# Linear attention and two expert layers on one core: w_in loaded in rows of 128, q and k by heads in two transfers each, two quarters of a product by TensorE transposes, and a new order

## The chip, the cores and the metric

The kernel runs on one core of a Trainium2 chip. The metric is the device time of one execution in microseconds (us). The engines are TensorE (PE in the rows; PEld is its weight load), VectorE (DVE), ScalarE (ACT), GpSimd (POOL) and SyncE (SP), whose instruction stream does nearly all the loading by issuing DMAs.

## What is computed

The reference has three stages, each fed by the one before it.

```python
# 1: linear attention with decay, B=2, H=8, S=768, D=64, in blocks of 64 rows
intra = einsum('bhic,bhjc->bhij', qb, kb) * Dmask        # Dmask[h,i,j] = lam[h]**(i-j), i >= j
out   = einsum('bhij,bhjd->bhid', intra, vb) + einsum('bhid,bhde->bhie', qb * lam_pow, kv_state)
kv_state = lam**64 * kv_state + einsum('bhsd,bhse->bhde', kb * rev_pow, vb)
x = out.transpose(0, 2, 1, 3).reshape(1536, 512)
# 2: w_in [512, 2048] and w_out [2048, 512] are float64
h = x @ w_in
y = (h * clip(h + 3, 0, 6) / 6) @ w_out                  # [1536, 512]
# 3: soft mixture: phi [512, 32], w1 [8, 512, 1024], w2 [8, 1024, 512]
logits = y @ phi                                         # 32 slots, 4 for each of 8 experts
slots  = softmax(logits, over tokens).T @ y
slot_out[e] = relu(slots[e] @ w1[e]) @ w2[e]
result = softmax(logits, over slots) @ slot_out          # [1536, 512]
```

## The kernel before

**Tiling.** The attention works on chunks of 128 rows: twelve tiles `t`, six for each of the two batches. For each tile `load_qkv` (L412 to L430, issue in L419) loads q and k side by side into one tile `qk` of 128 partitions x 2 x 8 heads x 64, and v into `vd`, with one DMA of 256 KB for each of q, k and v. TensorE transposes q and k by pairs of heads into `pt` (`f_tr`, L793, four products each), ScalarE evicts them to `tr` (`f_ev`, L810), TensorE makes the scores `ps` (`f_sc`, L862), VectorE multiplies them by the decay table `dec` into `pm` (`f_pm`, L870), and TensorE makes the outputs `px` (`f_px`, L900 and L907) and the state's increment `pv` (`f_pv`, L883). `px` becomes `x`, the transposed input of the second stage, split in a high and a low part. In `x` a block `kt` of 128 rows holds the heads `kt` and `kt + 4`.

**The float64 matrices.** A piece of w_in (`load_w_in`, L433 to L441, issue in L438) is 128 rows x 512 columns of 8 bytes, 512 KB, in a tile `wraw`; there are 16, for four quarters of columns and four blocks `kt`. Since block `kt` of `x` holds the heads `kt` and `kt + 4`, its rows of w_in are two runs of 64, and each piece comes by two DMAs of 64 partitions. ScalarE and VectorE convert each piece to float32 (`convert`, L583, L590, L597, L604, tiles `tmp_i`; the same code converts w_out, loaded by `load_wo_raw` in 16 pieces `wo_raw`, tiles `tmp_o`, into `wo_f`), and it is split into `whi` (ScalarE, L630) and `wlo` (VectorE or GpSimd, L633). The product `h` (L1019) has 48 groups, four quarters by twelve tiles, each of twelve products of 128x512, done in two halves of six. ScalarE (L1033) and VectorE (L1039) evict it to `g`.

**The product w2s.** w_out is not multiplied by `g`; first w_out times phi is formed, `w2s`, in four quarters (`make_w2s`). It needs w_out transposed, and there are two ways for a quarter, chosen by the tuple `w2dma`. Before, all four quarters are in it: VectorE transposes blocks of 32 (`wb`, L710, two for a quarter), four DMAs of 128 KB for each of these move the blocks between partitions (`wq`, L723), and TensorE makes 64 products `w2p` (L735). The other way, which no quarter takes before, is four groups of four transposes on TensorE (`pwo`), an eviction of each by ScalarE (`wo_t`) and 32 products of twice the columns. The logits `lg` (L1125) need `g` transposed and use the VectorE way with moves `gq` (L1102, L1112).

**The end.** Softmax terms (`lr`, `pd`) follow; then the experts' weights are streamed in 64 DMAs of 512 KB (`e`, L1322, L1332, L1346) for the products `p` (L1540) and `po` (L1574), and the result is combined.

**What sets the order.** Nothing is scheduled on the chip or by a planner. The program makes a list of numbered operations, and the table `ORDER` says in which order their code is run; each engine executes its instructions in that order, and waits where an operand is late. `Plan.run` also uses modelled times, but only to decide which free buffer an operation takes. Loads have 4-KB slots in a ring of 50; a few of the moves can be issued by ScalarE instead of SP, those numbered in `BY_ACT`. SP issues all loads of q, k, v, w_in, w_out and `e` and nearly all moves in one stream, a DMA waiting there when its buffer is not free or when eight transfers are under way. `keep_on` (L544) fills TensorE with products that nobody reads.

## Time and profile before

| | before |
|---|---|
| median of 3 runs | 309.9 us (309.62 to 311.62) |
| the profiled execution | 310.75 us |
| its span | 308.9 us |
| TensorE busy | 277.1 us, 90% |
| VectorE busy | 198.8 us, 64% |
| ScalarE busy | 122.8 us, 40% |
| GpSimd busy | 36.3 us, 12% |
| moved by DMA | 78.67 MB, mean 255 GB/s |
| chain that ended last | PE 63%, DMA 17%, SP's issues 10% |

The span is the time from the first to the last instruction that the profiler recorded, and the execution's own time lies 1.85 us above it. Busy shares are averages over the whole span. The clock that TensorE was granted (PEclk) is given as a share of full speed; its two levels are 1.2 and 2.4 GHz. The DMA share is how busy the 16 transfer engines were on average; it can show a little over 1 where packets overlap. The chain of work that ended last follows the last instruction back to what released it, step by step.

### The profile page before, as it was taken

To read this page: it belongs to the slowest core of one execution; us is meant where nothing else is said; L and a number is where in the kernel's file an instruction comes from. 1 tells how busy PE (TensorE), PEld (TensorE's weight loads), DVE (VectorE), ACT (ScalarE), POOL (GpSimd) and SP (SyncE) were. 2 spreads that over 40 slices of the span, in tenths; PEclk is the share of its full clock that TensorE was granted. 3 is DMA by queue.
4 is the path that set the end of the run, shared out by engine and by line. 5 is a ranking of instruction groups with operands and counts; after the bars stand their busy time and mean duration, and the time that the engine had idled before them with its cause. 6 is when DMAs were issued, how large, how long until landed. Compare 5 with 4: busy or idle time off the path is not lost.

```text
span 308.9 us, 7313 instructions
## 1 busy us (share of the span) xinstructions
PE 277.1 (90%) x2956; PEld 210.1 (68%) x2956; DVE 198.8 (64%) x330; ACT 122.8 (40%) x235; POOL 36.3 (12%) x51
## 2 busy tenths in 40 slices
PE   6269994999879899999999999999999998979990
PEld 5268883878657788788667768668776756556670
DVE  3368894799946999998987796675633216213151
ACT  3454555988347657312131232224124241111240
POOL 4034210423202602000110010100000000000000
PEclk9578998899959999999999999999999999999997
DMA  7999999999996765667896768999799999999987
GB/s 145 221 234 210 208 213 179 241 293 317 219 215 181 249 181 153 168 155 191 194 262 162 205 152 197 227 306 358 243 334 417 395 408 342 389 407 407 313 262 235
DMA packets 79217, 78.67 MB, mean 255 GB/s; under 512 B 41800, under 2 KB 67920, under 8 KB 79184
## 3 DMA queue, kind: packets, MB, share of 16 engines
q1 hardware_dynamic: 76704, 76.37, 88.1%
q10 hardware_dynamic: 2480, 1.84, 2.1%
q8 instruction: 23, 0.38, 0.5%
q14 instruction: 10, 0.08, 0.1%
HBM read 60.36 MB, written 3.15 MB: 206 GB/s over the span
## 4 chain that ended last, share of the span: by engine, by line
PE 63%; DMA 17%; SPq 10%; DVE 4%; issue 1%; ACT 1%; POOLq 0%; DVEq 0%; ACTq 0%
PE h L1019 35%; SPq L419 5%; SPq L438 4%; DMA wo_raw<-in_moe_w_out_dram 4%; PE po L1574 4%; DMA e<-in_moe_w_dram 4%; PE lg L1125 3%; DMA qk<-in_q_dram 3%; PE p L1540 3%; PE pd L1240 3%; PE ps L862 3%; DMA wraw<-in_moe_w_in_dram 2%; PE pt L793 2%; PE px L907 2%; DMA qk<-in_k_dram 2%; DMA gq<-gb 2%
## 5 line engine op out<-in xcount | busy, mean ns | idle before, releaser
L1019 PE MATMUL h<-whi,x 128*128 128x512 f32 x384 | 124.1, 405 | 0.6 <-DVE g L1039 0.6
L1019 PEld LDWEIGHTS h<-whi,x 128*128 128x128 f32 x384 | 70.8, 191 | 17.6 <-issue 2.0
L1019 PE MATMUL h<-wlo,x 128*128 128x512 f32 x192 | 75.9, 395 | 0.0
L1033 ACT ACTIVATE g<-h,half_b 128x512 f32<-128x512 f32 x48 | 33.0, 688 | 53.1 <-PE h L1019 37.4
L1039 DVE SCALAR_TENSOR_TENSOR g<-g,h 128x512 f32<-128x512 f32 x48 | 32.6, 678 | 29.3 <-ACT g L1033 25.9
L1102 DVE STREAM_TRANSPOSE gb<-g 128x1024 f32<-128x1024 f32 x20 | 40.9, 2053 | 5.3 <-POOL vd L849 2.5
L1019 PEld LDWEIGHTS h<-wlo,x 128*128 128x128 f32 x192 | 36.6, 191 | 8.3
L793 PE MATMUL pt<-ident,qk 128*128 128x128 f32 x96 | 15.8, 308 | 13.8 <-DMA qk<-in_q_dram 13.8
L793 PEld LDWEIGHTS pt<-ident,qk 128*128 128x128 f32 x96 | 12.1, 155 | 17.4 <-DMA qk<-in_q_dram 8.0
L931 POOL TENSOR_TENSOR states<-states,lamq 64x256 f32<-64x256 f32 x16 | 10.7, 669 | 88.9 <-DVE states L944 80.7
L810 ACT COPY tr<-pt 128x512 f32<-128x512 f32 x24 | 13.6, 582 | 17.9 <-PE pt L793 9.5
L870 DVE TENSOR_TENSOR pm<-ps,dec 128x512 f32<-128x512 f32 x24 | 15.7, 681 | 7.2 <-ACT tmp_o L590 4.0
L862 PE MATMUL ps<-tr 64*128 64x128 f32 x192 | 15.9, 306 | 3.2 <-ACT tr L810 3.0
L862 PEld LDWEIGHTS ps<-tr 64*128 64x128 f32 x192 | 13.3, 207 | 7.1 <-ACT tr L810 3.5
L583 ACT ACTIVATE tmp_i<-wraw 128x512 f32<-128x512 f32 x16 | 10.5, 670 | 18.9 <-DMA wraw<-in_moe_w_in_dram 14.5
L1559 DVE STREAM_TRANSPOSE ht<-hsi 128x256 f32<-128x256 f32 x8 | 5.1, 651 | 19.6 <-ACT hsi L1551 19.6
L1540 PE MATMUL p<-e,hsi 128*32 128x256 f32 x256 | 15.2, 381 | 2.1 <-DMA e<-in_moe_w_dram 1.6
L710 DVE STREAM_TRANSPOSE wb<-wo_f 128x1024 f32<-128x1024 f32 x8 | 16.1, 2022 | 0.1
L849 POOL TENSOR_TENSOR vd<-qk,rev 128x512 f32<-128x512 f32 x10 | 11.0, 1112 | 42.8 <-DVE rev L535 12.8
L1574 PE MATMUL po<-e,ht 128*32 128x128 f32 (+1 forms) x384 | 15.4, 309 | 0.3 <-DMA e<-in_moe_w_dram 0.3
L633 POOL TENSOR_TENSOR wlo<-tmp_i,whi 128x512 fp32r<-128x512 f32 x8 | 11.2, 1419 | 25.4 <-ACT whi L630 25.3
L1574 PEld LDWEIGHTS po<-e,ht 128*32 128x32 f32 x384 | 11.1, 110 | 4.4 <-DMA e<-in_moe_w_dram 0.5
(115 smaller groups left out, 341.9 us busy)
## 6 DMA issues: line engine op xcount, KB each, us to landing
e<-in_moe_w_dram SPq DMA_DIRECT2D x64, 512.0 KB, 7.1
gq<-gb SPq DMA_DIRECT2D x76, 128.0 KB, 2.8
wraw<-in_moe_w_in_dram SPq DMA_DIRECT2D x32, 256.0 KB, 6.6
wo_raw<-in_moe_w_out_dram SPq DMA_DIRECT2D x16, 512.0 KB, 6.0
wq<-wb SPq DMA_DIRECT2D x28, 128.0 KB, 2.7
qk<-in_k_dram SPq DMA_DIRECT2D x12, 256.0 KB, 5.8
...
```

The costliest lines, as they stand in the source:

```text
L419: QUEUE[plan.eng].dma_start(out=T[name, t][:, i], in_={"q": q, "k": k, "v": v}[x][b, :, C * c : C * c + C].rearrange("h p d -> p h d"),)
L710: DVE.transpose(out=x.rearrange("p q d c f -> p c d q f"), in_=y.rearrange("p c (d t q) -> p c d q t", d=KT, q=4),)
L793: PE.transpose(p[:, a], x[:, i, 2 * a : 2 * a + 2].rearrange("p a d -> p (a d)"), ident,)
L810: ACT.copy(T["tr", t][:, i], T["pt", t, i])
L862: PE.matmul(ps[g][:, p], lhsT=z[r, p], rhs=y[r, p], start=True, stop=True)
L870: DVE.tensor_tensor(out=T["pm", t].rearrange("p (a g) c -> p g a c", g=2)[:, g], in0=T["ps", t][g], in1=T["dec"].rearrange("p (a g) c -> p ...
L1019: PE.matmul(ph, lhsT=xt[:, a, kt], rhs=T[w, n, part][:, kt % 2], start=i == 0, stop=i == 3 * KT - 1,)
L1033: ACT.activation(T["g", tp, n][:, i], T["h", t, n], AF.Relu, bias=half_b, scale=1.0 / 6.0)
L1039: DVE.scalar_tensor_tensor(out=to, in0=to, scalar=1.0, in1=T.pop(("h", t, n)), op0=ALU.min, op1=ALU.mult,)
L1102: DVE.transpose(out=x.rearrange("p q c i t -> p i c q t"), in_=T["g", tp, n].rearrange("p i (c t q) -> p i c q t", c=4, q=4),)
L1540: PE.matmul(p1[32 * j : 32 * j + 32], lhsT=T["sit"][:, b4], rhs=T["e1", e, b4][:, 256 * j : 256 * j + 256], start=b4 == 0, stop=b4 == 3,)
L1574: PE.matmul(T["po", hf][32 * qd : 32 * qd + 32], lhsT=T["ht", e // 4][:, e % 4, b8], rhs=T["e2", e, b8 // 2][:, b8 % 2, lo:hi] if e < WHOL ...
```

## The change

The heads are laid out differently. `x` now holds the heads `2 kt` and `2 kt + 1` in block `kt`, so a piece of w_in is one run of 128 rows and comes by one DMA. The transposes of q and k, which take two neighbours in the tile at a time, must then pair the heads `h` and `h + 4`: these are put side by side in the tile of q or k, by two DMAs of 128 KB in place of one of 256 KB; v keeps its order. `rev`, `pm`, `pv`, `px` and the choice matrix `selp` follow the new order of heads. Quarters 1 and 3 of `w2s` take the TensorE way. The table of the order is a new one altogether, and so is `BY_ACT`. In the code after the change, lines lie 4 to 9 further down.

```diff
-    w2dma=(0, 1, 2, 3),
+    w2dma=(0, 2),
...
 ORDER = (
-    10, 0, 252, 253, 2, 9, 246, 248, 247, 73, 18, 6, 4, 76, 270, 254, 77, 255, 3, 271,
+    73, 0, 74, 76, 77, 75, 2, 9, 10, 246, 248, 247, 249, 250, 6, 4, 78, 79, 3, 80,
...
-BY_ACT = (421, 709, 885, 918, 939,)
+BY_ACT = (674, 697, 717, 926,)
...
@@ -351,7 +351,7 @@
     POOL.memset(selp, 0.0)
     POOL.affine_select(
         out=selp, in_=selp, compare_op=ALU.not_equal, fill=1.0,
-        base=0, pattern=[[-2, NPAIR], [-1, 2], [0, 64]], channel_multiplier=1,
+        base=0, pattern=[[-1, NPAIR], [-4, 2], [0, 64]], channel_multiplier=1,
     )
     sel = const.tile([128, 4, 32], F32, name="sel")
     POOL.memset(sel, 0.0)
@@ -416,16 +416,20 @@
         def fn():
             if (name, t) not in T:
                 T[name, t] = rtile([128, 2, H, D], f"{name}{t}")
-            QUEUE[plan.eng].dma_start(
-                out=T[name, t][:, i],
-                in_={"q": q, "k": k, "v": v}[x][b, :, C * c : C * c + C].rearrange(
-                    "h p d -> p h d"
-                ),
-            )
+            src = {"q": q, "k": k, "v": v}[x][b, :, C * c : C * c + C].rearrange("h p d -> p h d")
+            if x == "v":
+                QUEUE[plan.eng].dma_start(out=T[name, t][:, i], in_=src)
+                return
+            to = T[name, t][:, i].rearrange("p (a g) d -> p g a d", g=2)
+            for g in range(2):
+                QUEUE[plan.eng].dma_start(
+                    out=to[:, g], in_=src[:, NPAIR * g : NPAIR * g + NPAIR]
+                )
 
         take = [] if (name, t) in bufs else [ring_buf((name, t))]
         ops["ld" + x, t] = load(
             fn, KB512 / 2, take=take, rel=[] if take else [bufs[name, t]], eff=0.58, rows=64,
+            n=1 if x == "v" else 2,
             **queue(f"{x}{t}"),
             reserve=load_reserve,
         )
@@ -433,15 +437,15 @@
     def load_w_in(n, kt):
         def fn():
             T["wraw", n, kt] = rtile([128, 512, 2], f"wraw{n}_{kt}", I32)
-            for i in range(2):
-                r = D * (KT * i + kt)
-                QUEUE[plan.eng].dma_start(
-                    out=T["wraw", n, kt][D * i : D * i + D].rearrange("p f w -> p (f w)"),
-                    in_=w_in.bitcast(I32)[r : r + D, 1024 * n : 1024 * n + 1024],
-                )
+            QUEUE[plan.eng].dma_start(
+                out=T["wraw", n, kt].rearrange("p f w -> p (f w)"),
+                in_=w_in.bitcast(I32)[
+                    128 * kt : 128 * kt + 128, 1024 * n : 1024 * n + 1024
+                ],
+            )
 
         ops["ldw", n, kt] = load(
-            fn, KB512, take=[ring_buf(("wraw", n, kt))], reserve=load_reserve, eff=1.1, n=2,
+            fn, KB512, take=[ring_buf(("wraw", n, kt))], reserve=load_reserve, eff=1.1,
             **queue(f"w{n}_{kt}"),
         )
 
@@ -532,7 +536,10 @@
         PE.matmul(T["rev_p"], lhsT=rp[:, 0:C], rhs=ident[:32, :H], start=True, stop=True)
 
     def make_rev():
-        DVE.tensor_copy(rev, T.pop("rev_p"))
+        DVE.tensor_copy(
+            rev.rearrange("p (a g) -> p g a", g=2),
+            T.pop("rev_p").rearrange("p (g a) -> p g a", g=2),
+        )
 
     def make_lamq():
         T["lamq"] = rtile([128, NPAIR, C], "lamq")
@@ -868,9 +875,9 @@
                 if ("pm", t) not in T:
                     T["pm", t] = rtile([128, H, C], f"pm{t}")
                 DVE.tensor_tensor(
-                    out=T["pm", t].rearrange("p (a g) c -> p g a c", g=2)[:, g],
+                    out=T["pm", t].rearrange("p (g a) c -> p g a c", g=2)[:, g],
                     in0=T["ps", t][g],
-                    in1=T["dec"].rearrange("p (a g) c -> p g a c", g=2)[:, g], op=ALU.mult,
+                    in1=T["dec"].rearrange("p (g a) c -> p g a c", g=2)[:, g], op=ALU.mult,
                 )
 
             return fn
@@ -879,42 +886,44 @@
             vd = T["vd", t]
             pv = T["pv", t] = ptile(v_tag, [128, NPAIR, D], f"pv{t}")
             for h in range(H):
-                p, h2 = divmod(h, 2)
+                g, p = divmod(h, NPAIR)
                 PE.matmul(
-                    pv[64 * h2 : 64 * h2 + 64, p], lhsT=vd[:, 1, h], rhs=vd[:, 0, h],
+                    pv[64 * g : 64 * g + 64, p], lhsT=vd[:, 1, 2 * p + g], rhs=vd[:, 0, h],
                     start=True, stop=True,
                 )
 
         def bank(kt):
-            return T["px", t, kt % 2][:, kt // 2] if c > 0 else T["px", t, 0][:, kt]
+            return T["px", t, kt // 2][:, kt % 2] if c > 0 else T["px", t, 0][:, kt]
 
         def f_px():
             vd, P = T["vd", t], T["pm", t]
             T["px", t, 0] = ptile("x", [128, 2 if c > 0 else KT, C], f"px{t}_0")
             if c > 0:
                 T["px", t, 1] = ptile("g", [128, 2, C], f"px{t}_1")
-            for kt in range(KT if c > 0 else 0):
+            for kt in (0, 2, 1, 3) if c > 0 else ():
                 for i in range(2):
-                    p, h2 = divmod(KT * i + kt, 2)
-                    r = slice(64 * h2, 64 * h2 + 64)
+                    g, p = divmod(2 * kt + i, NPAIR)
+                    r = slice(64 * g, 64 * g + 64)
                     PE.matmul(
                         bank(kt)[64 * i : 64 * i + 64], lhsT=old[r, p, r],
-                        rhs=T["trd", t][r, p], start=kt < 2, stop=False,
+                        rhs=T["trd", t][r, p], start=kt % 2 == 0, stop=False,
                     )
             for kt in range(KT):
                 for i in range(2):
-                    h = KT * i + kt
+                    h = 2 * kt + i
                     PE.matmul(
                         bank(kt)[64 * i : 64 * i + 64], lhsT=vd[:, 0, h], rhs=P[:, h],
-                        start=c == 0, stop=c == 0 or kt >= KT - 2,
+                        start=c == 0, stop=c == 0 or kt % 2 == 1,
                     )
 
         def parts():
             x = T["x", t]
             if c == 0:
                 return [(x[:, 0], x[:, 1], T["px", t, 0])]
-            y = x.rearrange("p w (a b) c -> p w a b c", b=2)
-            return [(y[:, 0, :, b], y[:, 1, :, b], T["px", t, b]) for b in range(2)]
+            return [
+                (x[:, 0, 2 * b : 2 * b + 2], x[:, 1, 2 * b : 2 * b + 2], T["px", t, b])
+                for b in range(2)
+            ]
 
         def f_xh():
             T["x", t] = rtile([128, 2, KT, C], f"x{t}", F32R)
```

The table decides most of what changes place, and its numbers say nothing to a reader. So here are two places in SP's stream and one in TensorE's.

SP, the start of the program before the change, from the second DMA on. A row is a source line, the tile that is written with the number of its making, the source, the shape, and how many alike follow each other. `pw_d` and `dec` are the store of the powers of lambda and the two loads of the decay table that is built from them:

```order
L438 DMA wraw_1_128<-in_moe_w_in_dram 64x1024 x2
L419 DMA qk_134<-in_k_dram 128x8x64
L438 DMA wraw_0_136<-in_moe_w_in_dram 64x1024 x2
L438 DMA wraw_0_152<-in_moe_w_in_dram 64x1024 x2
L469 DMA pw_d<-rp 8x256
L419 DMA qk_134<-in_q_dram 128x8x64
L419 DMA qk_168<-in_k_dram 128x8x64
L438 DMA wraw_3_187<-in_moe_w_in_dram 64x1024 x2
L438 DMA wraw_2_203<-in_moe_w_in_dram 64x1024 x2
L419 DMA qk_168<-in_q_dram 128x8x64
L476 DMA dec<-pw_d 128x4x128 x2
L419 DMA vd_221<-in_v_dram 128x8x64
```

The same place after the change:

```order
L425 DMA qk_147<-in_k_dram 128x4x64 x2
L440 DMA wraw_0_150<-in_moe_w_in_dram 128x1024
L440 DMA wraw_1_152<-in_moe_w_in_dram 128x1024
L473 DMA pw_d<-rp 8x256
L425 DMA qk_147<-in_q_dram 128x4x64 x2
L425 DMA qk_172<-in_k_dram 128x4x64 x2
L425 DMA qk_172<-in_q_dram 128x4x64 x2
L440 DMA wraw_2_185<-in_moe_w_in_dram 128x1024
L421 DMA vd_194<-in_v_dram 128x8x64
L480 DMA dec<-pw_d 128x4x128 x2
L440 DMA wraw_3_232<-in_moe_w_in_dram 128x1024
```

The first k and two pieces of w_in are issued first, `dec` stands behind three pieces of w_in in place of five and ahead of the fourth, and v's first load has moved ahead of `dec`.

SP, from the third v to the loads of the sixth and seventh tile before the change (`qk_388` and `qk_398`; of the sixth only q is loaded here). TensorE's wait that ends at 52.80 us is for the q of `qk_388`:

```order
L419 DMA vd_288<-in_v_dram 128x8x64
L419 DMA qk_292<-in_k_dram 128x8x64
L419 DMA qk_292<-in_q_dram 128x8x64
L438 DMA wraw_3_310<-in_moe_w_in_dram 64x1024 x2
L438 DMA wraw_2_316<-in_moe_w_in_dram 64x1024 x2
L438 DMA wraw_0_338<-in_moe_w_in_dram 64x1024 x2
L419 DMA vd_341<-in_v_dram 128x8x64
L438 DMA wraw_0_362<-in_moe_w_in_dram 64x1024 x2
L438 DMA wraw_2_366<-in_moe_w_in_dram 64x1024 x2
L419 DMA qk_388<-in_q_dram 128x8x64
L419 DMA qk_398<-in_q_dram 128x8x64
L419 DMA qk_398<-in_k_dram 128x8x64
```

The same stretch after the change, up to the fifth tile `qk_412`, whose transposes now stand where those of `qk_388` stood in TensorE's stream:

```order
L440 DMA wraw_1_271<-in_moe_w_in_dram 128x1024
L425 DMA qk_275<-in_k_dram 128x4x64 x2
L425 DMA qk_275<-in_q_dram 128x4x64 x2
L440 DMA wraw_2_307<-in_moe_w_in_dram 128x1024
L421 DMA vd_327<-in_v_dram 128x8x64
L440 DMA wraw_0_329<-in_moe_w_in_dram 128x1024
L440 DMA wraw_3_351<-in_moe_w_in_dram 128x1024
L440 DMA wraw_3_353<-in_moe_w_in_dram 128x1024
L421 DMA vd_355<-in_v_dram 128x8x64
L440 DMA wraw_0_386<-in_moe_w_in_dram 128x1024
L425 DMA qk_412<-in_k_dram 128x4x64 x2
L425 DMA qk_412<-in_q_dram 128x4x64 x2
```

TensorE asks for the fifth tile there in place of the sixth, and one tile's q and k fewer stand ahead. Between `dec` and that tile stand seven pieces of w_in in one DMA each, where six stood in two each.

TensorE, around the first `w2p`, before the change (`w2p` is one quarter of `w2s`, `wq` the moved blocks of w_out):

```order
L1019 MATMUL h_0_1070<-whi_2_313,x_916 128x512 x2
L1019 MATMUL h_0_1070<-wlo_2_314,x_916 128x512
L735 MATMUL w2p_1087<-wq_0_978,phi_b 32x64 x16
L735 MATMUL w2p_1087<-wq_1_985,phi_b 32x64 x16
L900 MATMUL px_0_1130<-trd_646,states 64x128 x2
L900 MATMUL px_1_1131<-trd_646,states 64x128 x2
L900 MATMUL px_0_1130<-trd_646,states 64x128 x2
L900 MATMUL px_1_1131<-trd_646,states 64x128 x2
```

And after it, two of the four groups of transposes of a quarter of the other kind, with the halves of `h` behind them:

```order
L688 MATMUL pwo_1_1126<-ident,wo_f_952 128x128 x2
L688 MATMUL pwo_1_1126<-ident,wo_f_784 128x128 x2
L1028 MATMUL h_2_1132<-whi_0_1054,x_279 128x512 x2
L1028 MATMUL h_2_1132<-wlo_0_1055,x_279 128x512
L1028 MATMUL h_2_1132<-whi_0_1054,x_279 128x512 x2
L1028 MATMUL h_2_1132<-wlo_0_1055,x_279 128x512
L688 MATMUL pwo_3_1143<-ident,wo_f_952 128x128 x2
L688 MATMUL pwo_3_1143<-ident,wo_f_784 128x128 x2
L1028 MATMUL h_2_1132<-whi_2_844,x_279 128x512 x2
L1028 MATMUL h_2_1132<-wlo_2_845,x_279 128x512
L1028 MATMUL h_2_1132<-whi_2_844,x_279 128x512 x2
L1028 MATMUL h_2_1132<-wlo_2_845,x_279 128x512
```

Each group of four transposes (two rows x2) stands between halves of `h`, and the 32 products of the quarter come later; there are eight such groups in all, four for each of the two quarters. On VectorE the transposes into `wb` go from eight to four, and the moves into `wq` from 32 (28 by SP, 4 by ScalarE) to 16, all by SP. Of the 80 moves `gq` ScalarE issues 12 in place of 4. In SP's stream 13 of the 64 loads of `e` stood ahead of the last move of a `gq`; now 10 do.

## Rows read from the trace of the kernel before

**Rows 1.** Stretches: columns named in its first line, for TensorE's regimes
```profile
core 0: us, PE busy (x) PEld busy (x) DVE busy (x) ACT busy (x) POOL busy (x), PEclk, DMA share, GB/s
20.00:100.00 80.00, 71.41 (x623) 58.42 (x624) 62.67 (x106) 52.11 (x94) 18.10 (x18) 0.91 1.03 229
20.90:27.40 6.50, 6.43 (x68) 6.02 (x68) 4.68 (x9) 3.72 (x8) 1.19 (x2) 0.74 1.34 227
60.00:80.00 20.00, 20.00 (x187) 16.07 (x184) 19.27 (x32) 18.24 (x33) 6.95 (x7) 1.00 1.10 295
102.60:251.00 148.40, 148.20 (x1317) 108.96 (x1317) 106.66 (x145) 48.70 (x96) 10.62 (x12) 1.00 0.82 246
52.00:56.00 4.00, 3.20 (x12) 2.70 (x13) 1.46 (x3) 1.85 (x5) 0.00 (x0) 0.57 0.83 199
```

**Rows 2.** TensorE's timeline: start, duration, then the instructions and the idle time before
```profile
28.33 0.71 PE L1019 MATMUL h<-whi,x 128*128 128x512 f32 x2
...
48.49 0.64 PE L883 MATMUL pv<-vd 128*64 128x64 f32 x16
52.80 2.09 PE L793 MATMUL pt<-ident,qk 128*128 128x128 f32 x8 [3.67 <-DMA qk<-in_q_dram]
...
87.15 2.08 PE L862 MATMUL ps<-tr 64*128 64x128 f32 x16 [3.05 <-ACT tr L810]
89.16 1.22 PE L1019 MATMUL h<-whi,x 128*128 128x512 f32 x2
...
93.17 0.67 PE L1019 MATMUL h<-whi,x 128*128 128x512 f32 x2
```

**Rows 3.** The chain of work that ended last: start, us, what, instructions
```profile
74.04 11.81 DMA wo_raw<-in_moe_w_out_dram
...
104.72 0.58 PE pt L793 x4
105.31 9.58 PE h L1019 x42
114.88 0.44 PE pt L793 x4
...
124.89 1.03 PE w2p L735 x64
```

**Rows 4.** DMAs of w_in, line L438, issued from 13 to 14 us
```profile
L438 SPq DMA_DIRECT2D wraw<-in_moe_w_in_dram x2: 595/595/595, 12.7 to 13.3; - x2
...
DMA to landing us min/median/max: 5.9/6.1/6.3
```

**Rows 5.** DMAs of the weights `e`, issued from 267 to 279 us
```profile
L1332 SPq DMA_DIRECT2D e<-in_moe_w_dram x8: 327/328/328, 267.3 to 278.8; - x8
L1322 SPq DMA_DIRECT2D e<-in_moe_w_dram x2: 327/328/328, 271.2 to 273.7; - x2
...
DMA to landing us min/median/max: 10.1/10.1/10.4
```

**Rows 6.** The first DMA of w_in, line L438, issued at 1.2 us
```profile
L438 SPq DMA_DIRECT2D wraw<-in_moe_w_in_dram x1: 576/576/576, 1.2 to 1.2; - x1
...
DMA to landing us min/median/max: 4.0/4.0/4.0
```

**Rows 7.** DMAs of the decay table `dec`
```profile
L476 SPq DMA_DIRECT2D dec<-pw_d x2: 505/543/581, 14.6 to 15.2; - x2
...
DMA to landing us min/median/max: 7.5/7.5/7.5
```

**Rows 8.** The page's costliest groups: block transposes of w_out on VectorE
```profile
L710 DVE STREAM_TRANSPOSE wb<-wo_f 128x1024 f32<-128x1024 f32 x8 | 16.1, 2022 | 0.1
```

**Rows 9.** DMAs of 128 KB into `wq`, issued from 113 to 116 us
```profile
L723 SPq DMA_DIRECT2D wq<-wb x4: 543/611/1221, 113.3 to 115.2; - x4
...
DMA to landing us min/median/max: 3.3/3.8/4.1
```

**Rows 10.** TensorE's waits by line: us in total, times, longest
```profile
PE p L1540 <- DMA e<-in_moe_w_dram: 1.6, 1, 1.6
```

94 rows, old and new, of the table ORDER are left out of this document.

## Prediction, made before the changed kernel was run

> **What bounds the kernel now.** I read the share by engine in a few stretches first, then TensorE's timeline for the places where it stands still, then the landing times of single transfers, and last the chain of work that ended last. The stretches [rows 1] say that there are three regimes. From 102.6 to 251 us TensorE is busy 148.2 of 148.4 us at the full clock: it is the bound there, and whatever VectorE or the queues save in that stretch is worth nothing by itself. From 20 to 100 us TensorE is busy 71.4 of 80 us, although its clock and its work are the same, with VectorE at 62.7; the 16 transfer engines are full (share 1.03) and move only 229 GB/s. After 251 us the weights of the second block stream in.
>
> What TensorE waits for shows in its timeline [rows 2]. The first product of `h`, from which it runs densely, starts at 28.33. At 52.80 it comes back from 3.67 us of waiting for a `q`, at 87.15 from 3.05 us of waiting for an eviction of ScalarE. Both times it comes back at half the clock (granted 0.57 from 52 to 56 us [rows 1], the lower of the two levels for most of it). What that costs is read beside rows at the full clock: after the first, eight transposes take 2.09 us where four take 0.44 to 0.58 [rows 3], so 1.1 too much; after the second, nine products of `h` take 4.01 us (89.16 to 93.17, 0.446 each) for the 2.06 that 0.228 each makes (42 in 9.58 us [rows 3]), and of the 2.08 of the sixteen scores before them I put a little under half to the clock, together 2.9. At 0.446 the first three products after the first stall lose another 0.6, so 1.7 there. So the two stalls cost 5.4 and 5.9 us. The second one's eviction stood behind a conversion on ScalarE that waited for a `wo_raw`, which landed 11.81 us after its issue [rows 3]: again the transfers.
>
> **The rate of the pieces of w_in.** Two 64-row pieces of 256 KB, issued at 12.7 and 13.3, landed 5.9 and 6.3 us later, so 1.1 us apart [rows 4]: a whole 512-KB piece takes 2.2 us. The nearest row with 128 rows of 4 KB from a matrix with a 16-KB row pitch, which is what the change makes of w_in, is that of `e`: ten issues, eight and two of the two lines, from 267.3 to 278.8 with a constant landing time, so nine steps of 1.28 us for 512 KB [rows 5]. The q, k and v pieces of 256 KB go at 227 GB/s [rows 1], 1.15 us each. I take 1.28 us for a piece of w_in (ends: 1.28, and 2.2 if the number of rows is not the reason), a saving of 0.92 each, 14.7 us over the 16 pieces, all of it in the full stretch.
>
> The row alone does not say that the 64 rows are the reason, since q with its 128 rows is as slow. The Trainium skill ("SBUF — State Buffer", Door 1: The DMA port swizzle) says that partitions 0 to 63 reach 8 of the 16 ports, 218 GB/s against 436 at most. By its two figures a piece would take an estimated 2.4 and 1.2 us, a saving of 1.2 in place of 0.92, and the two terms below that rest on it would grow by about a third; the trace agrees with the low figure (238 GB/s) and I stay with its rows.
>
> **The head.** Landings by the order shown: a first 256 KB landed at 5.2, issued at 1.2 with 4.0 to landing [rows 6]; then two pieces of w_in (2.56), q0, k1, q1 (3.45), a piece of w_in (1.28), v0 (1.15) and `dec` (2.3) give 16.0. Before, `dec` landed at 15.2+7.5=22.7 [rows 7], behind five pieces of w_in. From there to the first `h` it was 5.6 us, of which 1.15 is v0, one transfer behind `dec`; v0 now stands ahead, which leaves 4.5. So `h` starts at 20.5 in place of 28.3: **-7.8**. With 2.2 us per piece, `dec` lands at 18.8 and `h` starts at 23.3: -5.0 by the order alone.
>
> **The first stall.** From 28.33 to the end of the product row at 48.49+0.64=49.1 [rows 2], TensorE did seven halves of `h` (six products each), four groups of transposes, and the products of three tiles: 20.8 us. In the new order there is one half (1.37) and one group (0.44) less before the transposes that stand in that place, now those of the fifth tile's q4 and k4 (`qk_412`): 19.0 us, at 39.5. After `dec`, seven pieces of w_in (9.0) and nine of q, k and v (10.35) bring k4 and q4 in at 35.3. A margin of 4 us covers it; with 2.2 us per piece they land at 44.5 against 42.3. So the stall goes: **-5.4** (ends 0 and -5.4).
>
> **The second stall.** By SP's order the `wo_raw` that was waited for stands between two pieces of w_in ahead of it and one behind it, which share the transfer engines with it: three at 0.92 give back 2.8 of the 3.05 us of waiting, and the clock's 2.9 go with it. But ScalarE's conversions still stand in order ahead of evictions, 16 times for `wo_raw`, and one can be late elsewhere. Ends 0 and -5.9; I take **-4.5**, nearer the end that the arithmetic gives.
>
> **The transposes.** Two quarters of w2s now cost 8 groups of four on TensorE, each 0.44 to 0.58 us, as the same groups for q and k cost there [rows 3]: 3.5 to 4.7, **+4.0**, in a stretch that TensorE bounds, so nothing hides it. The products behind them stay at about 1.03 us per quarter (the row of `w2p` [rows 3]; half as many products of twice the columns). The 8 evictions on ScalarE hide under TensorE (48.7 busy of 148.4 us [rows 1]); if that cover failed they would cost 8 times some 0.6. VectorE loses four transposes of 2.02 us [rows 8] and the queues 16 moves: worth nothing where TensorE is full. I give them no credit, but they pay for VectorE's tighter time below.
>
> **The halves of q and k.** 24 more transfers of 128 KB. Four transfers of that size landed 0.4 us apart when they queued (113.3+4.1=117.4 to 115.2+3.3=118.5 [rows 9]), less than half of 1.15. SP needs about 0.6 us to issue one: 17 issues up to the last piece of w_in's first quarter are some 10.5 us against landings up to 17.3, so it keeps ahead. Cost 0; upper end in the third rival.
>
> **The tail.** The loads of `e` land 1.28 apart when they queue [rows 5]. Before, 13 of the 64 stand ahead of the last move of a `gq` on SP, now 10, so three more (3.8 us) come behind the same place. TensorE waits for `e` in that stretch once, for 1.6 us [rows 10], so stream and products are nearly level: I take half, **+1.9** (ends 0 and 3.8).
>
> Sum: -7.8-5.4-4.5+4.0+1.9=-11.8. The profiled execution took 310.75 us (span 308.9), 0.85 above the median of 309.9, so 298.95 for it and **298.1** as a median.
>
> **Rivals.**
> 1. The new order finds its own waits. In 60 to 80 us VectorE is busy 19.27 and ScalarE 18.24 of 20 us [rows 1]. Closing the gaps of the 80 us up to 100 squeezes VectorE's 62.7 us of work (58.7 without two transposes of w2) into some 63. If it can only be filled to 90%, 65.2 us are needed, and conversions in order behind transfers add as much: +4.4, **302.5**. For it: both engines are full where TensorE is. Against: TensorE had no gap in that very stretch.
> 2. The piece's rate does not change, because something else holds the head to 230 GB/s. Then the head gives -5.0, the first stall shrinks by 1.4 (2.2 of its wait left, and the clock), the second stays, and +5.9 remain: -0.5, **309.4**. For it: q with 128 rows is as slow. Against: those are 256-byte pieces, and `e` with this very pattern runs at 400 GB/s.
> 3. Slower: a half of q or k takes as long as a whole (1.15), because a transfer has a cost that doesn't shrink. Place: SP's queue, 24 times. Four of them ahead of `dec` bring `h` to 25.1 (-3.2), ten put k4 and q4 at 46.8 against 44.1 (2.7 us of waiting, and the clock's 1.7, stay), so 1.0 of it is gained, the second stall stays, and six more ahead of it add 6.9: -3.2-1.0+6.9+5.9=+8.6, **318.5**. It decides against the change from some 0.7 us for each added transfer (11.8 of the 20.4 us between this sum and the forecast's, of 1.15). Against it: the 0.4 us [rows 9]. The Trainium skill speaks for it ("SBUF — State Buffer", The DMA setup-cost knee): every transfer pays about 2 us that do not scale with its bytes. By that rule, were it paid in the stream and not beside it, 24 halves would be an estimated 48 us; the trace's spacing speaks against that.
> 4. Better: the second stall goes wholly, and half of the transposes fall into waits that remain elsewhere, and the stream of `e` starts early enough: -7.8-5.4-5.9+2=-17.1, **292.8**.
>
> **How the numbers follow.** Forecast 0.55, rival 1 0.22, rival 2 0.08, rival 3 0.06, rival 4 0.09. The predicted time is the forecast's, 298.1. Leaving out rival 3 and the outer parts of rivals 2 and 4 gives 290 to 307 for 8 in 10; the likeliest case alone spans 293 to 302. About 1% (3.1 us) is what a measurement of this kernel can tell from no change: faster by more, under 306.8, is the forecast, rival 4 and nearly all of rival 1: 0.85; within it 0.09; slower, over 313, 0.06.
>
> **What would show it.** Right: a piece of w_in lands about 1.3 us after the one before; the first `h` near 20.5 us; no wait for a `q` near 40 to 50 us; the 8 groups of transposes at 0.44 to 0.58 us each inside a full TensorE. Wrong: pieces of w_in still 2.2 us apart (rival 2); halves of q 1 us apart (rival 3); VectorE above 95% from 20 to 90 us with TensorE waiting for it (rival 1); a gapless stream of `e` that ends as late as before although TensorE's last `h` is 15 us earlier, which would make the tail's term too small.

## The result and the profile after

The changed kernel takes 301.28 us in the median (297.69 to 303.55, four runs) where the kernel before takes 310.76 beside it; the ratio is 0.965 (95% interval 0.953 to 0.976), so it is faster by 3.5%. The ratio leaves out the slowest of the four runs, 303.55, which was in a slower state. The prediction was 298.1, with a range from 290 to 307. The profiled execution of the changed kernel took 297.69 us (span 295.8); the sum of the prediction gave 298.95 for such an execution. That is near, but several terms of the sum were off and cancel. The median lies 3.2 us above the forecast, and by e7 one wait that the prediction did not have costs the median about 4 us. The experiments below find both.

The stretches of the changed kernel, with the columns of [rows 1]; the first and the second line answer to the lines of the same stretches there:

```profile
core 0: us, PE busy (x) PEld busy (x) DVE busy (x) ACT busy (x) POOL busy (x), PEclk, DMA share, GB/s
20.00:100.00 80.00, 79.12 (x701) 64.50 (x700) 71.03 (x119) 63.16 (x111) 21.66 (x21) 1.00 0.83 244
60.00:80.00 20.00, 19.49 (x141) 15.64 (x140) 17.09 (x35) 17.35 (x30) 3.72 (x3) 1.00 0.60 173
100.00:200.00 100.00, 100.00 (x972) 73.91 (x971) 77.90 (x106) 28.44 (x61) 6.80 (x9) 1.00 0.73 186
200.00:240.00 40.00, 37.26 (x255) 27.04 (x254) 11.82 (x23) 12.87 (x27) 0.00 (x0) 1.00 0.95 352
```

TensorE is now busy 79.1 of the 80 us up to 100, where it was busy 71.4, and the transfer engines are no longer full (0.83 for 1.03). VectorE and ScalarE are busy 71.0 and 63.2 us there, 8 to 11 more than before, since work that lay behind has come forward.

TensorE's timeline of the changed kernel, with the columns of [rows 2]. The first line is the first product of `h`, the second the transposes of the fifth tile, which wait for nothing; then come all the waits of 0.25 us and more up to 240 us, and the products `psi` that follow the softmax sums, with the products `p` behind them:

```profile
19.40 0.71 PE L1028 MATMUL h<-whi,x 128*128 128x512 f32 x2
...
39.04 1.09 PE L800 MATMUL pt<-ident,qk 128*128 128x128 f32 x8
...
60.77 0.73 PE L1028 MATMUL h<-whi,x 128*128 128x512 f32 x2 [0.51 <-DVE g L1048]
...
86.07 0.66 PE L688 MATMUL pwo<-ident,wo_f 128*128 128x128 f32 x4 [0.28 <-ACT wo_t L696]
...
216.60 1.07 PE L1134 MATMUL lg<-gq,w2s 128*32 128x256 f32 x16 [2.24 <-DMA e<-in_moe_w_dram]
...
243.84 1.08 PE L1421 MATMUL psi<-wo_f,ant 128*32 128x128 f32 x32
...
244.79 2.80 PE L1421 MATMUL psi<-wo_f,ant 128*32 128x128 f32 x94
249.71 0.41 PE L1421 MATMUL psi<-wo_f,ant 128*32 128x128 f32 x2 [2.11 <-issue]
251.05 3.66 PE L1549 MATMUL p<-e,hsi 128*32 128x256 f32 x64 [0.94 <-PE psi L1421]
```

`h` starts at 19.40 in place of 28.33. From there on there is no wait for a q, and none for an eviction `tr`. What remains up to 200 us are 0.51 and 0.28. Two things are new: 2.24 us ahead of the products `lg` at 216.60, and 2.11 us up to 249.71, ahead of the last two of `psi`, for which the profile shows no releaser. `psi` starts 13.5 us earlier than before, and the span ends 13.1 us earlier. The same line before the change:

```profile
257.30 1.08 PE L1412 MATMUL psi<-wo_f,ant 128*32 128x128 f32 x32 [0.46 <-ACT ant L1383]
```

### The profile page after: what moved, and what is told of

It is laid out like the page before. It is cut to its first block, busy times and chain, and to the rows that moved or that the text cites. A ratio compares the mean times of both kernels' runs of the same rounds, so it can differ in the third digit from the quotient of the medians.

```text
span 295.8 us, 7251 instructions
## 1 busy us (share of the span) xinstructions
PE 278.5 (94%) x2924; PEld 213.1 (72%) x2924; DVE 191.6 (65%) x326; ACT 126.6 (43%) x243; POOL 35.3 (12%) x51
## 4 chain that ended last, share of the span: by engine, by line
PE 75%; DMA 10%; DVE 8%; ACT 3%; issue 2%; SPq 0%; DVEq 0%; ACTq 0%
PE h L1028 34%; PE p L1549 5%; PE po L1583 5%; PE ps L869 4%; PE lg L1134 4%; PE pt L800 3%; PE pd L1249 3%; PE px L914 3%; DMA wo_raw<-in_moe_w_out_dram 3%; DMA wraw<-in_moe_w_in_dram 2%; PE pv L890 2%; DMA e<-in_moe_w_dram 2%; DMA gq<-gb 2%; PE px L907 2%; PE pt L1652 2%
## 5 line engine op out<-in xcount | busy, mean ns | idle before, releaser
L1028 PE MATMUL h<-whi,x 128*128 128x512 f32 x384 | 121.7, 398 | 0.5 <-DVE g L1048 0.5
L1028 PEld LDWEIGHTS h<-whi,x 128*128 128x128 f32 x384 | 69.7, 188 | 16.1 <-issue 1.6
L1028 PE MATMUL h<-wlo,x 128*128 128x512 f32 x192 | 75.0, 391 | 0.0
L1028 PEld LDWEIGHTS h<-wlo,x 128*128 128x128 f32 x192 | 36.0, 188 | 7.8
L800 PE MATMUL pt<-ident,qk 128*128 128x128 f32 x96 | 14.8, 292 | 1.5 <-DMA qk<-in_q_dram 1.5
L869 PEld LDWEIGHTS ps<-tr 64*128 64x128 f32 x192 | 12.5, 199 | 3.6 <-issue 2.1
L869 PE MATMUL ps<-tr 64*128 64x128 f32 x192 | 14.9, 297 | 0.1
L611 DVE SCALAR_TENSOR_TENSOR tmp_i<-tmp_i 128x512 int32<-128x512 int32 x16 | 11.9, 761 | 3.2 <-ACT tmp_i L597 2.6
L611 DVE SCALAR_TENSOR_TENSOR wo_f<-tmp_o 128x512 int32<-128x512 int32 x16 | 13.5, 852 | 0.5 <-ACT tmp_o L597 0.2
L1549 PEld LDWEIGHTS p<-e,hsi 128*32 128x32 f32 x256 | 8.6, 110 | 7.2 <-issue 1.3
```

The source lines that it names most:

```text
L611: DVE.scalar_tensor_tensor(out=lw if dst is None else dst(), in0=hp, scalar=3, in1=lw, op0=ALU.logical_shift_left, op1=ALU.bitwise_or,)
L800: PE.transpose(p[:, a], x[:, i, 2 * a : 2 * a + 2].rearrange("p a d -> p (a d)"), ident,)
L869: PE.matmul(ps[g][:, p], lhsT=z[r, p], rhs=y[r, p], start=True, stop=True)
L1028: PE.matmul(ph, lhsT=xt[:, a, kt], rhs=T[w, n, part][:, kt % 2], start=i == 0, stop=i == 3 * KT - 1,)
L1549: PE.matmul(p1[32 * j : 32 * j + 32], lhsT=T["sit"][:, b4], rhs=T["e1", e, b4][:, 256 * j : 256 * j + 256], start=b4 == 0, stop=b4 == 3,)
```

## The experiments

Each was timed several times beside the kernel before, which took 310.2 to 311.4 us in the median. The places inside a kernel are read from one profiled execution each; in the two of the changed kernel `psi` starts 0.8 us apart (243.84 and 244.67), so smaller differences there mean little.

| run | what differs | median us (range) | ratio to before (95%) |
|---|---|---|---|
| e1 | the changed kernel again | 301.52 (299.57 to 303.30) | 0.971 (0.964 to 0.977) |
| e2 | changed, w_in by 64 rows | 317.42 (316.03 to 319.58) | 1.023 (1.016 to 1.029) |
| e3 | new loads, old order, no transposes for w2s | 296.55 (295.40 to 298.08) | 0.955 (0.949 to 0.961) |
| e4 | as e3, w_in by 64 rows | 311.11 (309.44 to 312.59) | 1.001 (0.997 to 1.004) |
| e5 | changed, transposes for w2s twice | 303.17 (300.54 to 305.67) | 0.970 (0.966 to 0.975) |
| e6 | changed, w_in by half columns | 303.61 (301.14 to 303.91) | 0.977 (0.972 to 0.982) |
| e7 | changed, one move of a `gq` ahead of two `e` | 297.28 (296.58 to 298.41) | 0.958 (0.955 to 0.962) |
| e8 | new head, old order behind it | 303.62 (302.66 to 304.21) | 0.978 (0.975 to 0.982) |
| e9 | e7, transposes for w2s twice | 298.38 (297.78 to 300.39) | 0.962 (0.956 to 0.968) |
| e10 | e8, one conversion later | 295.15 (294.56 to 300.42) | 0.949 (0.943 to 0.954) |
| e11 | e7, all of w2s by VectorE | 309.71 (308.90 to 310.33) | 0.994 (0.991 to 0.997) |
| e12 | e7, 64 instructions more on TensorE | 296.70 (295.46 to 298.89) | 0.955 (0.949 to 0.960) |

### The rate of w_in: e1, e2 and e6

> The changed kernel once more, unchanged, so that the other kernels of this group have it beside them. Four executions lay between 297.7 and 303.6 us; the theory (the one of the prediction) and its rivals expect the same here, a median of 300 to 302.

It took 301.52. e2 changes only how a piece of w_in comes:

```diff
-            QUEUE[plan.eng].dma_start(out=T["wraw", n, kt]..., in_=w_in[128 * kt : 128 * kt + 128, ...])
+            for i in range(2):
+                r = 128 * kt + D * i
+                QUEUE[plan.eng].dma_start(out=T["wraw", n, kt][D * i : D * i + D]..., in_=w_in[r : r + D, ...])
```

> The changed kernel with each piece of w_in in two DMAs of 64 rows again (rows 0 to 63 and 64 to 127 of the tile), all else kept. Theory (the number of partitions sets the rate): a piece takes 2.2 us again, the first h starts near 22.5 us in place of 19.6, TensorE waits for a q again before 50 us, total 306 to 311 (rival 2 of the prediction worked out 309.4 for this). Rival (the new order and not the rate brings the gain): a piece still lands in about 1.4 us, or lands later without TensorE waiting, total 300 to 303.

It took 317.42: 16 us more than the changed kernel, 7 more than before the change, and above the range that was expected. e6 has as many transfers of as many bytes, but all 128 rows in each:

```diff
+            for i in range(2):
+                c = 1024 * n + 512 * i
+                QUEUE[plan.eng].dma_start(out=T["wraw", n, kt][:, half i], in_=w_in[128 * kt : 128 * kt + 128, c : c + 512])
```

> The changed kernel with each piece of w_in in two DMAs of 256 KB again, but each of 128 rows by half of the columns (2 KB in a row), so as many transfers, and as many bytes in each, as with 64 rows. Theory (64 partitions were the reason for the low rate): near the changed kernel, 300 to 305, a pair landing in 1.3 to 1.6 us. Rival (the number of transfers or their size is the reason): near the 317 us of the kernel with 64 rows.

It took 303.61. So it is the number of rows that counts, not the count or the size of the transfers. DMAs of w_in that queue behind each other, in the changed kernel (512 KB each), in e2 and in e6 (256 KB each); the landing times lie in order of the issues:

```profile
L440 SPq DMA_DIRECT2D wraw<-in_moe_w_in_dram x2: 430/430/430, 23.7 to 24.1; - x2
...
DMA to landing us min/median/max: 6.9/7.3/7.8
```

```profile
L442 SPq DMA_DIRECT2D wraw<-in_moe_w_in_dram x4: 589/594/595, 30.5 to 32.4; - x4
...
DMA to landing us min/median/max: 7.8/8.5/9.2
```

```profile
L442 SPq DMA_DIRECT2D wraw<-in_moe_w_in_dram x3: 430/430/827, 24.3 to 25.7; - x3
...
DMA to landing us min/median/max: 4.4/4.6/4.7
```

The spacing of the landings is that of the issues plus the difference of the landing times. In the changed kernel it is 0.5 us between issues and 0.9 between the landing times, 1.4 us for 512 KB. In e2 it is (1.9+1.4)/3=1.1 us for 256 KB, as before the change, so 2.2 for a piece. In e6 it is (1.4+0.1)/2, some 0.75, so 1.5. With half the rows a piece takes 2.2 us in place of 1.4; shorter rows cost little, if anything.

e2 is also the test of rival 2, which had 309.4. `h` starts at 23.75, as the working of that rival had it (23.3), and there is a wait for a q near 50 us, of 3.39 where it left 2.2. But TensorE also waits where the rival priced nothing: 1.69 us for an eviction `tr` at 36.95, 1.32 and 1.97 for a `g` at 67.96 and 77.29, and 3.59 ahead of a product `lg` at 236.09. The start of `h` and the wait for the q:

```profile
23.75 0.71 PE L1028 MATMUL h<-whi,x 128*128 128x512 f32 x2
...
50.77 1.32 PE L800 MATMUL pt<-ident,qk 128*128 128x128 f32 x8 [3.39 <-DMA qk<-in_q_dram]
```

### The old order with the new loads: e3 and e4

Both use the old table, the old moves by ScalarE and `w2dma=(0, 1, 2, 3)`; e4 has w_in in 64-row transfers besides.

```diff
-    w2dma=(0, 2),
+    w2dma=(0, 1, 2, 3),
-ORDER = (73, 0, 74, 76, ...)          # the changed kernel's
+ORDER = (10, 0, 252, 253, ...)        # that of the kernel before
```

> The new loads with the order of before: w_in in one DMA of 128 rows, q and k in two by heads, but the old table, the old moves by ScalarE and all four quarters of w2s by VectorE and moves. Theory: five pieces ahead of dec give back 0.92 us each, so h starts near 23.7 us in place of 28.3 (-4.6), the wait for the sixth q goes (-5.4), the second stall mostly (-4.5), and no transposes (+4.0) are paid: 295 to 300. Rival (the loads save little until the order is written for them, since the same waits stand in the same places): 303 to 308.

> As the kernel with the new loads and the old order, but w_in in two DMAs of 64 rows: against the kernel before only the layout of heads and the halves of q and k are new. Theory (a half costs half): 308 to 312, as before. Rival 3 of the prediction (each added transfer costs up to 0.6 to 1.15 us): 316 to 325.

e3 took 296.55, as the theory had it and 5 us less than the changed kernel; e4 took 311.11, like the kernel before. So the 128-row transfers alone are worth 14.6 us in the old order (e4 to e3) and 15.9 in the new one (e2 to e1). The new order and the transposes together cost 5 us in the median (4 of them lie in one move, as e7 below shows), although `h` starts 4.5 us earlier than in e3:

```profile
23.91 0.71 PE L1028 MATMUL h<-whi,x 128*128 128x512 f32 x2
```

That e4 equals the kernel before does not by itself show that the halves of q and k are free, because its parts cancel. `h` starts 1.5 us later, and the first stall is nearly gone, as TensorE comes there about 2 us later and q is there by then. The second stall stands as before (the third line; 3.05 us there):

```profile
29.79 0.71 PE L1028 MATMUL h<-whi,x 128*128 128x512 f32 x2
...
52.09 0.63 PE L800 MATMUL pt<-ident,qk 128*128 128x128 f32 x4 [0.27 <-DVE g L1048]
...
85.41 2.08 PE L869 MATMUL ps<-tr 64*128 64x128 f32 x16 [3.18 <-ACT tr L817]
```

In e3, where only the rows of w_in differ from e4, this stall is gone. So the rate of the pieces took it away, and not the new order.

What answers rival 3 is the spacing of two halves of the first q in the changed kernel, 0.4 us between the issues and 0.1 between the landing times, so 0.5 for a half, where a whole took 1.15:

```profile
L425 SPq DMA_DIRECT2D qk<-in_q_dram x2: 378/445/512, 5.1 to 5.5; - x2
...
DMA to landing us min/median/max: 3.1/3.2/3.2
```

### A part of the change that nobody priced: the products pv

`f_pv` has the same sixteen products per tile as before, by their own row 0.22 us each. Their line in the stretch from 100 to 240 us at the full clock, before (four tiles) and after (three tiles); busy time with the number of products is the second column:

```profile
100.00:240.00 140.00, 2.54 (x64) 2.41 (x64) 1.00 0.80 231
```

```profile
100.00:240.00 140.00, 2.75 (x48) 2.65 (x48) 1.00 0.79 234
```

A tile's sixteen take 0.635 us before and 0.917 after, 0.28 more. There are ten such tiles, nine of them behind the first `h`, so 2.5 us of TensorE, which bounds those stretches. The new table is not the reason: e4 keeps the old one, and its four tiles in that stretch take 0.915 each.

```profile
100.00:240.00 140.00, 3.66 (x64) 3.53 (x64) 1.00 0.79 227
```

So it comes with the new layout of the heads. The diff shows what changed there: before, neighbouring heads wrote to the lower and the upper 64 partitions of the output by turns; now four heads in a row write to one half. That the turns are the reason is argued from the diff. No run put them back, so it is not shown.

### The new wait ahead of lg: e7, and e5 beside it

The four DMAs of the move that TensorE waited for at 216.60, issued by ScalarE in the changed kernel:

```profile
L1121 ACTq DMA_DIRECT2D gq<-gb x4: 551/626/628, 206.4 to 208.3; - x4
...
DMA to landing us min/median/max: 5.0/6.1/8.1
```

They land 5.0 to 8.1 us after their issue, the last one, issued at 208.3, just ahead of 216.5, among loads of `e` of 512 KB which SP issued around them. When the last was issued, SP had issued 16 loads of `e`. (The row of TensorE's wait names a load of `e` that landed at about the same time; what the products read is `gq`.) e7 gives them to SP and puts them ahead of two of these loads:

```diff
-    ..., 780 (load e), ..., 802 (load e), 592, 717 (move gq, by ScalarE), 596, ...
+    ..., 592, 717 (move gq, by SP), 780 (load e), 802 (load e), 596, ...
-BY_ACT = (674, 697, 717, 926,)
+BY_ACT = (674, 697, 926,)
```

> The changed kernel with one move of a gq (four DMAs of 128 KB) taken from ScalarE to SP and put ahead of two loads of e that were issued before it. In the changed kernel these four landed 5.0 to 8.1 us after their issue, among the loads of e, and TensorE waited 1.7 to 2.2 us for the last. Theory: that wait goes, the stream of e is 2 us later at that place and has caught up by the end: 299 to 300.5. Rival (the stream of e bounds the end, so what TensorE gains there it waits for later): 301 to 303.

It took 297.28, 4 us less than the changed kernel, below the range that was expected, and it spreads less: 296.6 to 298.4 in place of 299.6 to 303.3. e7 changes the engine that issues the move and its place at once, so it does not say which of the two counts.

The wait explains about half of the 4 us: `psi` starts at 241.56 in place of 243.84. In the profiled pair even that is lost again behind `psi` (297.38 and 297.69 in all), as will be seen below. Where the rest of the gain in the median comes from is not shown; the clock is a candidate. In the two profiled executions of the changed kernel the wait was 2.24 and 1.68 us, and the sixteen products behind it took 1.07 us. Where it was longer, TensorE came back at the lower clock; e5, which has the same move in the same place:

```profile
222.53 1.94 PE L1135 MATMUL lg<-gq,w2s 128*32 128x256 f32 x16 [3.28 <-DMA gq<-gb]
```

Those products take 1.94 us there, and the granted clock from 222.4 to 224.6 us is 0.50, the lower level (columns as in [rows 1]):

```profile
222.40:224.60 2.20, 2.07 (x17) 0.89 (x18) 0.00 (x0) 0.00 (x0) 0.00 (x0) 0.50 0.52 195
```

The same products took 1.94 us behind a wait of 2.92 in e6 and 1.93 behind one of 3.59 in e2. The unprofiled executions of the changed kernel had a mean granted clock of 0.968 to 0.975 where the profiled, fastest one had 0.991. That they lost it behind this wait fits, but their traces were not kept. In e1 the profiled execution has 0.977 in all, and yet the full clock behind this wait, so a low mean does not point to this place by itself. It is inferred, not shown.

### The price of the transposes: e5, e9 and e11

```diff
-                for c in range(4):
+                for c in range(8):
+                    c = c % 4
                     x = T["wo_f", 2 * n + c // 2].bitcast(F32)[:, c % 2]
                     PE.transpose(p[:, c], x[:, 128 * dt : 128 * dt + 128], ident)
```

> The changed kernel with each of the eight groups of four transposes of w_out done twice into the same place, so with eight groups more. Theory (TensorE bounds that stretch, nothing hides a group): 8 x 0.44 to 0.66 us more, so 3.5 to 5.3 above the changed kernel's 301.5, 305 to 307. Rival (the groups fall into waits that are there anyway, so the gain that the old order with the new loads has over the changed kernel does not come from them): 301 to 303.

It took 303.17, only 1.7 above the changed kernel, and lies between the two ranges. The total could not tell the two theories apart, since it also holds the wait ahead of `lg`, now 3.28 us with the clock, and the idle time in `psi`, now gone. e9 does the same on e7, which has no such wait:

> The kernel with the move of the gq put ahead (297.3 us), with each of the eight groups of transposes of w_out done twice, so 64 more instructions (32 products and their 32 weight loads) on TensorE. Theory on the groups (nothing hides them in a stretch that TensorE bounds): TensorE reaches the products psi 8 x 0.44 to 0.58 = 3.5 to 4.6 us later (243.2 to 244.3 us after the start of psi's first product at some 239.7 to 241.5 in that kernel). Theory on the idle 1.9 to 2.2 us between psi's last two products (it hangs on the place in TensorE's instruction stream, not on data): it is gone, as in the first kernel with double groups, and with it the half clock after it, so the total grows by 0.5 to 2 us only, 297.5 to 299.5. Rival (the idle time hangs on data that come late): it stays, and the total is 300.5 to 302.

It took 298.38. `psi` starts at 244.80 in place of 241.56, so the eight groups cost 3.24 us, 0.41 each, a little less than the 3.5 that was expected (the first `h` starts at 19.53 and 19.64, so the heads are alike). The idle time in `psi` is gone, and the total is only 1.1 above e7: the theory holds on both points.

e11 takes the groups out and gives the two quarters back to VectorE:

```diff
-    w2dma=(0, 2),
+    w2dma=(0, 1, 2, 3),
-    ..., eight transposes pwo on TensorE, eight evictions on ScalarE, ...
+    ..., four transposes wb on VectorE, four moves wq (16 DMAs) on SP, at about the same places, ...
```

> The new order with the move of the gq put ahead (297.3 us), but all four quarters of w2s by VectorE and moves: the eight groups of transposes and their evictions are taken out, four transposes wb of 2.0 us on VectorE and 16 moves come in at about the same places, and the products of the first of these quarters stand four halves of h later. Theory (the groups cost TensorE 0.4 us each and VectorE has room for 8 us more from 80 to 130 us): psi starts 3.3 us earlier than the 241.6 us of that kernel, the idle time between psi's last products goes too, since 64 more instructions stand ahead of them, and the total is 292 to 294.5. Rival (VectorE has no room, which is why the new order gave these quarters to TensorE): TensorE waits for a g, a pm or a w2p between 75 and 130 us, total 296 to 300.

It took 309.71, 12 us more than e7 and far above both ranges. Its two longest waits of TensorE:

```profile
88.46 1.22 PE L1028 MATMUL h<-whi,x 128*128 128x512 f32 x2 [3.65 <-DVE g L1048]
...
136.08 0.96 PE L1134 MATMUL lg<-gq,w2s 128*32 128x256 f32 x8 [4.71 <-DVE w2s L711]
```

TensorE waits for VectorE's `g` seven times, 8.5 us in all, and 4.7 for the `w2s` of a quarter. But these rows do not mean that VectorE is full: from 80 to 100 us it is busy 15.73 us, and 17.88 in the changed kernel. Ahead of the first of the two waits VectorE itself stands idle for 4.00 us, for an eviction by ScalarE, which stands idle for 7.01 us until moves `wq` have landed. Ahead of the second VectorE is idle for 2.34 us, again for moves `wq`:

```profile
87.00 0.69 ACT L1042 ACTIVATE g<-h,half_b 128x512 f32<-128x512 f32 x1 [7.01 <-DMA wq<-wb]
87.72 0.69 DVE L1048 SCALAR_TENSOR_TENSOR g<-g,h 128x512 f32<-128x512 f32 x1 [4.00 <-ACT g L1042]
...
130.63 1.99 DVE L1111 STREAM_TRANSPOSE gb<-g 128x1024 f32<-128x1024 f32 x1 [2.34 <-DMA wq<-wb]
```

So the moves that the VectorE way needs are late at the two longest waits. A shorter one, of 1.35 us at 99.50, stands right behind a transpose `wb` of 2.05 us on VectorE. Why ScalarE has to wait for the moves the rows do not say. e11 is one choice of places: it shows that this work does not fit there, not that VectorE has no time for it, and not that no place exists. The changed kernel has a stretch without slack too: its chain of work that ended last leaves TensorE for 24 us, for two transfers and the conversions behind them, though TensorE itself waits only 0.51 us at the end of it (columns as in [rows 3]):

```profile
36.89 7.04 DMA wraw<-in_moe_w_in_dram
...
43.95 7.54 DMA wo_raw<-in_moe_w_out_dram
...
60.11 0.61 DVE g L1048
```

### The new head on the old order: e8 and e10

e8 takes the first 67 operations of the new order and then the old order, on the loads of e3.

> The new loads with the head of the new order (its first 67 operations, up to the first product of h) and the old order from there, all four quarters of w2s by VectorE. Theory (the new order's head is worth 4 us and its rest loses more than that): h starts near 20 us in place of 23.9, and the 296.6 us of the old order become 292 to 294. Rival (TensorE then runs ahead of VectorE, ScalarE or the loads, and the 4 us come back as waits): 295 to 298.

It took 303.62, 7 more than e3 and above both ranges. At 30.35 us TensorE comes back from 7.1 us of waiting for an eviction by ScalarE:

```profile
30.35 2.15 PE L869 MATMUL ps<-tr 64*128 64x128 f32 x16 [7.10 <-ACT tr L817]
```

Ahead of that eviction stands the conversion of a piece of w_in that the old order loads among the first four and the new head does not. e10 moves this one conversion behind the evictions.

```diff
-    ..., 18 (load piece), 270, 271, 272, 273 (its conversion), ..., 274, ..., 275, ..., 456, 277, ...
+    ..., 18 (load piece), ..., 456, 270, 271, 272, 273, 274, 275, 277, ...
```

> As the kernel with the new head and the old rest, but the conversion of the one piece of w_in that the head loads late (first piece of the second quarter) is moved behind the evictions of the third and fourth tile on ScalarE and VectorE; in the kernel before this one TensorE waited 7.1 us for such an eviction. Theory (only that conversion ate the head's 4 us): no wait above 1 us between 20 and 40 us, h starts near 20 us, 292 to 294. Rival (the old order's rest has no room for an earlier start, another wait comes up): 295 to 299.

It took 295.15 in the median, the lowest of all, with one of four executions at 300.42. It is 1.4 below e3, not 4, and the intervals of the two ratios overlap, so that even this is not sure: `h` starts 3.5 us earlier, but `psi` only 1.0 (242.17 for 243.18). The start of `h` and two waits that e3 doesn't have in this size:

```profile
20.39 0.71 PE L1028 MATMUL h<-whi,x 128*128 128x512 f32 x2
...
35.16 1.25 PE L800 MATMUL pt<-ident,qk 128*128 128x128 f32 x8 [1.02 <-DVE pm L877]
...
141.65 0.63 PE L800 MATMUL pt<-ident,qk 128*128 128x128 f32 x4 [1.21 <-DMA qk<-in_k_dram]
```

So neither theory holds whole: the conversion's place cost e8 its 7.1 us of waiting, but without it most of the earlier start comes back as other waits, as the rival had it.

### The idle time in psi: e12

In the changed kernel and in e2, e6 and e7, which have the same TensorE instructions, `psi` stops for 1.7 to 2.2 us ahead of its last products. In e5 and e9, with 64 instructions more ahead, it doesn't. Counted in the traces, 4189 instructions of TensorE (products and weight loads) lie ahead of `psi` in the five kernels that have the stop, and 4249 or 4253 in the nine that don't, the kernel before among them. e7:

```profile
241.56 1.08 PE L1421 MATMUL psi<-wo_f,ant 128*32 128x128 f32 x32
...
242.51 2.80 PE L1421 MATMUL psi<-wo_f,ant 128*32 128x128 f32 x94
247.24 0.41 PE L1421 MATMUL psi<-wo_f,ant 128*32 128x128 f32 x2 [1.93 <-issue]
248.59 5.19 PE L1549 MATMUL p<-e,hsi 128*32 128x256 f32 x64 [0.94 <-PE psi L1421]
```

The 64 products `p` behind it take 5.19 us (granted clock 0.70 from 248.6 to 253.8); in the changed kernel above they took 3.66 (1.00 from 251 to 255), so the lower clock follows this stop in one execution and not in the other, though the stop is no shorter there (2.11 for 1.93). e12 puts 64 instructions in where TensorE waits for the first q anyway:

```diff
         T["rev_p"] = ptile("h", [128, H], "rev_p")
+        for _ in range(17):
+            PE.matmul(T["rev_p"][0:32], lhsT=ident[:, 0:32], rhs=ident[:, 0:H], start=True, stop=True)
-        for _ in range(CFG["fill"]["first"]):
+        for _ in range(CFG["fill"]["first"] - 1):
```

> The kernel with the move of the gq put ahead (297.3 us), with 17 very small products (32 x 8) put in and one of the warming products taken out near 5 us, where TensorE waits for the first q anyway: 64 more instructions stand ahead of psi, at no other cost. Theory (the idle 1.9 us between psi's last products hangs on the place in TensorE's instruction stream): it is gone, and with it the 1.5 us that the half clock costs in the products after it; h and psi start within 0.5 us of that kernel's 19.6 and 241.6 us, total 294 to 296. Rival (the idle time hangs on the transposes of w_out being doubled or on what comes late with them): it stays, 297 to 298.5.

It took 296.70, above the 294 to 296 that were expected. The stop is gone:

```profile
243.39 1.08 PE L1423 MATMUL psi<-wo_f,ant 128*32 128x128 f32 x32
...
244.35 2.85 PE L1423 MATMUL psi<-wo_f,ant 128*32 128x128 f32 x96
248.14 2.80 PE L1551 MATMUL p<-e,hsi 128*32 128x256 f32 x48 [0.94 <-PE psi L1423]
```

But the small products were not free: `h` starts at 21.24 in place of 19.64 and `psi` 1.8 us later, so that the span from the start of `psi` to the end falls from 53.9 to 51.4 us and the total by 0.6 only, which the spread of the runs does not tell from nothing. That the stop hangs on the place in the instruction stream is shown. Why is not. A transfer of the instruction queue lies near it, in the changed kernel inside `psi` and half a microsecond ahead of the stop, in e12 at the start of `psi`, in e5, which has no stop, 0.4 us behind that start (one line each from a quarter of a microsecond from 247.0 in the changed kernel and from 243.25 in e12; packets, MB, share of the transfer engines):

```profile
q8 instruction: 1, 0.02, 26.9%
```

```profile
q8 instruction: 1, 0.02, 27.0%
```

## Why the prediction was right, and where it was not

**The rate of w_in** (right). 1.4 us per piece where 1.28 was taken, 2.2 with 64 rows. The rule of the Trainium skill ("SBUF — State Buffer", Door 1: The DMA port swizzle) agrees: e6 against e2 shows that the partitions and not the count of transfers set the rate, and the 2.2 and 1.4 us lie inside the estimated 2.4 and 1.2 that its figures give. The two pairs of runs found 14.6 and 15.9 us for the sixteen pieces, where the prediction worked out 14.7 of transfer time. That these are so near is in part luck: by the measured rates the transfer time is 16 times 0.8, 12.8 us, and the totals hold TensorE's waits and its clock besides.

**The head** (right): -7.8 forecast, `h` at 20.5; it started at 19.40, -8.9. `dec` landed at 16.0, just as worked out (9.3 and 10.0 to the issue, 5.9 to 6.0 to landing); the 1.1 us more lie between `dec` and `h`, 3.4 us where 4.5 was taken. e10 shows that in the old order such a start is worth less to the end than it looks.

**The stalls** (right, one too small). The wait for the q is gone, -5.4, and TensorE comes to the fifth tile's transposes at 39.04, as worked out (39.5). The second stall is gone wholly, -5.9 for the -4.5 taken, and by e3 and e4 for the reason given. Three small waits of before, together 1.9 us, went with them and were in no term.

**The transposes** (right, a little high): +4.0 forecast, 3.2 measured by e9 against e7.

**The halves** (right): nothing forecast, 0.5 us each in the stream.

**Missed: the products pv**, +2.5 behind the first `h`. The prediction has no term for `f_pv`, whose products are as many and as large as before. The step that failed is that the new layout was taken to cost TensorE nothing; e4 shows that it costs 0.28 us a tile in the old order too.

**Mis-sized: the tail.** It had +1.9 because fewer loads of `e` stand ahead of the last move. From `psi` to the end the profiled execution took 52.0 us, before 51.6: +0.4, and that with a stop of 2.11 us in `psi` which no term had; in e9 and e12, without the stop, it is 51.2 and 51.4. TensorE waits for no `e` behind `psi` in the changed kernel, so what the term feared did not come. The term counted SP's stream alone, 10 loads ahead of SP's last move of a `gq`. But the last move is now one of ScalarE's, and SP had issued 16 loads by then, where 13 stood ahead of the last move before. So the loads of `e` cost time at the other end: they are early and delay a move, 2.24 us ahead of `lg`, and by e7 some 4 us in the median. This is rival 1 in kind, a wait that the new order brings, but at another place than the one it named: a move between transfers, not VectorE. VectorE's tightness, its reason, is not what the rows show, neither in the changed kernel (0.51 us for a `g`) nor at the two longest waits of e11.

The sum for the profiled execution up to `psi`: -8.9-5.4-5.9-1.9+3.2+2.5+2.2+0.5+0.3=-13.4 against -13.5 measured; with the tail -13.0 against -13.1. The forecast's -11.8 came close to it because what it missed on either side was nearly equal, which is luck: 6.7 us better than forecast (head, second stall, small waits, transposes, tail) and 5.5 worse (`pv`, the wait ahead of `lg`, the two small new waits). Rival 2 was out by 8 us (309.4 for 317.4 in e2): it priced the head and the two stalls of before, and with slow pieces TensorE waits in more places.
